# Twelve weight sets made by a fixed plan, and partial sums requested one job ahead, in a retention, GLU and expert kernel

## The chip, the cores and the metric

One core of one Trainium2 chip. The metric is the device time of one execution in microseconds (us). The kernel before has a median of 2044.2 us over three runs (2042.75 to 2045.66).

## The reference, cut to what matters

```
attn = (scale * q @ k.T * decay) @ v                    # 4 batches, 8 heads, 576 x 64
x = rmsnorm(attn rows) * rms_g                          # 2304 tokens x 512
x = (silu(x @ w_gate) * (x @ w_val)) @ w_out            # 512 -> 1536 -> 512
P = exp(x @ moe2_w_gate - max); 8 rounds of row and column scaling
out = sum over 8 experts e of P[:, e] * (relu(x @ w1[e]) @ w2[e])   # 512 -> 1024 -> 512
```

Everything is float32. A product of two float32 matrices is made of three TensorE products of fp32r halves: a value is split into `hi` (a cast on ScalarE) and `lo` (value minus `hi`, on VectorE or GpSimd), and hi x hi, hi x lo and lo x hi are summed in PSUM.

## The kernel before

There are three stages: retention (up to about 80 us), the gated layer (GLU) and the experts (from about 563 us to the end).

**GLU.** The 1536 hidden columns go in six sweeps (`s` = 0 to 5, lines 710 to 754), 256 columns each. A sweep runs over five blocks of tokens (`BLOCKS`: three of 512, two of 384), and a block is a generator of five steps `i` (`gated_block`, line 186): i = 0 gate of the first 128 columns and its silu (L203, ScalarE); i = 1 their val product, the multiply (L209, VectorE), the split of the result (`ghi` L210 on ScalarE, `glo` L211 on VectorE); i = 2 and i = 3 the same for the second 128 columns; i = 4 the output product (`x`), which TensorE does for the first 128 columns and then for the second, and its addition to `acc` (L232, VectorE). One step is twelve products in i = 0 to 3 and 24 in i = 4. After each step the loop lets other work put a piece into the queues: `step_weights` (the GLU's own weights) and `late_steps`.

**Late weight sets.** In the expert stage the weights are read from DRAM in a prepared form: seven 256-wide blocks (four of the matrix, sums and differences for a Strassen-like scheme of seven products), each as hi and lo. There are UJ = 32 such jobs per unit of tokens (8 experts x 4 pairs of column blocks), for w1 and for w2. Jobs 0 to 19 make theirs as they go. Those of jobs LATE = 20 to 31, twelve of them, are made during GLU sweeps by `late_weights` (line 666), which calls `prepared` (line 626), a generator of five steps: step 0 casts three raw blocks to hi in two staging buffers (`high`, L631, ScalarE); step 1 makes lo (L636, VectorE) and stores hi and lo to DRAM (L643, on SP's DMA queue); step 2 makes four sums and differences in place in the raw tile (L653, GpSimd); step 3 casts them into the same staging buffers; step 4 makes lo and stores (L640 or L643). After step 4 the raw tile is free, and the raw matrix of the next job is loaded into it (L668, SP's queue).

Call one turn of `late_steps` a place: 25 places in a sweep, five in a block. Before, the w1 generator (x) and the w2 generator (y) of a job take eight places: x at 0, 1, 2, 4, 5 and y at 2, 3, 4, 6, 7, and the next job starts eight places on. The loads lie at places 5 (x) and 7 (y), three places ahead of their use. While the plan starts a job in sweep 1, x and y share one pair of staging buffers; the second pair (`staging[2:4]`) belongs to GLU weights until that sweep is over. Twelve jobs end at place 95; `late_steps` is called in sweeps 1 to 4, 100 times.

**Experts.** Tokens go in three units of 768 (`u`), 32 jobs each (`n`). In unit 0 the first 20 jobs, which are five experts, work in another layout (token rows); their sums are stored in DRAM as six tiles `part_kept`. From job 20 on, jobs go through the loop at lines 162 onward of the last part (1162 to 1281), with an order written out by hand; results of the second layer are gathered transposed in `acc_d`. When a unit is over, `finish_unit` (line 1139) does one of its six 128-token tiles in each of the next six jobs (`next(finishing)`, line 1227): TensorE transposes four 128 x 128 blocks into the PSUM bank `qx` (L1144). For unit 0, SP requests the stored sum of that tile into `part`, a piece of the SBUF tile `o_second` (L1146), and VectorE adds it to the bank (L1152) into `st`; for unit 1 ScalarE copies the bank (L1156). SP stores `st` (L1157). A few products later in the same job, `first(m, 1)` (L1076) writes the bank `qx` again. VectorE, ScalarE, TensorE and SP each work in program order. On SP's queue a job has, in order, `load_w1(n + 1)` (line 1166), the pieces of `load_w2(n)` (L1056), the `part` load, the `st` store.

Of the kernel before, what the change touches and what calls it, by code (L numbers as in the profile page):

```python
# [43 lines left out]
NCH = UNIT // 128  # L44
NPAIR = FE // 256
UJ = E * NPAIR
ROUTED = NPAIR + 2
LATE = 20

@with_exitstack
def retention_glu_experts(ctx: ExitStack, tc: tile.TileContext, a, out):
# [6 lines left out]
    nc = tc.nc  # L60
# [24 lines left out]
    def f32(t):  # L85
        return t.bitcast(F32)


    sources, staging = [], []
# [160 lines left out]
    at, views = 0, []  # L250
# [190 lines left out]
    for pr in range(NP):  # L441
        for hh in (2 * pr, 2 * pr + 1):
            nc.gpsimd.tensor_mul(mask_rows[:, hh, :], causal, g_in[:, hh:hh + 1].to_broadcast([128, C]))
        step = steps[:, pr].rearrange("p (d c) -> p d c", c=NC)[:, :, 1:]
# [78 lines left out]
    jobs = [(u, e, g) for u in range(NU) for e in range(E) for g in range(NPAIR)]  # L523
    raw1, raw2 = {}, {}
    w1_kept = [kept.tile([128, 3584], F32, tag=f"w1_{n}", name=f"w1_kept{n}") for n in range(UJ)]
    w2_kept = [kept.tile([128, 3584], F32, tag=f"w2_{n}", name=f"w2_kept{n}") for n in range(UJ)]
    prob_kept = kept.tile([E, NT], F32, tag="prob_t", name="prob_kept")
    part_kept = [kept.tile([128, DM], F32, tag=f"part{t}", name=f"part_kept{t}") for t in range(NCH)]

    def load_job(n):  # L530
        if n < LATE:
            _, e, g = jobs[n]
# [90 lines left out]
            split(u, name, x, nc.gpsimd if name != "S2" else nc.vector)  # L623
            yield

    def prepared(n, a_n, dst, raw_tile, stages, order, places, signs):
        w = raw_tile.rearrange("p (b f) -> p b f", f=256)
        kept_n = dst.rearrange("p (s b f) -> p s b f", s=2, f=256)

        def high(i, blocks):  # L630
            nc.scalar.copy(stages[i][0][:, :blocks.shape[1] * 256].rearrange("p (b f) -> p b f", f=256), blocks)  # L631

        def low(i, blocks, at):
            size = blocks.shape[1] * 256
            hi, lo = (t[:, :size].rearrange("p (b f) -> p b f", f=256) for t in stages[i])
            nc.vector.tensor_sub(lo, blocks, f32(hi))  # L636
            for s, t in enumerate((hi, lo)):
                if at[-1] < at[0]:
                    for b, place in enumerate(at):
                        nc.sync.dma_start(kept_n[:, s, place, :], f32(t)[:, b, :])  # L640
                else:
                    step = at[-1] - at[0] or 1
                    nc.sync.dma_start(kept_n[:, s, at[0]:at[-1] + 1:step, :], f32(t))  # L643

        first, (pair_a, pair_b) = order
        high(0, w[:, 0:2, :])
        high(1, w[:, 2:3, :])
        yield
        low(0, w[:, 0:2, :], (first, first + 1))
        low(1, w[:, 2:3, :], (first + 2,))  # L650
        yield
        for o, x, y in signs:
            nc.gpsimd.tensor_sub(w[:, o, :], w[:, x, :], w[:, y, :])  # L653
        yield
        blocks = [w[:, p[0]:p[1] + 1:p[1] - p[0], :] for p in (pair_a, pair_b)]
        for i in range(2):
            high(i, blocks[i])
        yield
        for i in range(2):
            low(i, blocks[i], places[i])  # L660
        yield

    W1_SUMS = (0, ((0, 1), (2, 3))), ((3, 6), (4, 5)), ((0, 3, 0), (3, 2, 3), (2, 2, 0), (1, 1, 2))
    W2_SUMS = (4, ((0, 2), (1, 3))), ((3, 0), (1, 2)), ((2, 3, 2), (3, 1, 3), (1, 1, 2), (0, 0, 1))

    def late_weights():
        def load(t, src):
            nc.sync.dma_start(t, src)  # L668

        for n in range(LATE, UJ):  # L670
            _, e, g = jobs[n]
            if n == LATE:
                load(ahead_raw[0], a["w1"][e, g])
                load(ahead_raw[1], a["w2"][e, g])
                yield
            second_stage = staging[2:4] if now[0] > 1 else staging[:2]
            x = prepared(n, a["w1"], w1_kept[n], ahead_raw[0], staging[:2], *W1_SUMS)
            y = prepared(n, a["w2"], w2_kept[n], ahead_raw[1], second_stage, *W2_SUMS)
            more = n + 1 < UJ
            next(x)  # L680
            yield
            next(x)
            yield
            next(x)
            next(y)
            yield
            next(y)
            yield
            next(y)
            next(x)  # L690
            yield
            next(x)
            if more:
                load(ahead_raw[0], a["w1"][jobs[n + 1][1:]])
            yield
            next(y)
            yield
            next(y)
            if more:
                load(ahead_raw[1], a["w2"][jobs[n + 1][1:]])  # L700
            yield

    ahead_raw, now = [], [0]
    late_steps = late_weights()
    scored = logits()
    first_unit = first_operands(
# [2 lines left out]
    first_job = first_weights(0)  # L709
    for s in range(NSWEEP):  # L710
        last_sweep = s == NSWEEP - 1
        now[0] = s
        if s == 1:
            norm_pool.close()
            ahead = glu.enter_context(tc.tile_pool(name="ahead", bufs=1, side="right"))
            ahead_raw += [ahead.tile([128, 1024], F32, name="ahead_raw"), tp.tile([128, 1024], F32, tag="lg", name="ahead_raw_2", bufs=1)]
            staging += [(shared_tiles[0][:, 4096:], shared_tiles[1][:, 3072:]), (shared_tiles[1][:, 2048:2560], shared_tiles[1][:, 2560:3072]), *more_slots[:2]]
            next(late_steps)
        for j, (t0, n) in enumerate(BLOCKS):
            last = j == len(BLOCKS) - 1  # L720
            block = gated_block(s, t0, n, last, pmm, pac, hp, tp, 1 if last_sweep and last else KD, 512)
            first_norms = not s and j + 1 < B
            assert s or (t0 + n - 1) // S in normed
            for i in range(2 * SWEEP + 1):
                if last_sweep and last and i == 2 * SWEEP:
                    break
                if first_norms and j and not i:
                    next(norms[j + 1])
                if i == 2 * SWEEP:
                    step_weights()  # L730
                next(block)
                if first_norms:
                    for _ in range((1, 1, 1, 2, 0)[i]):
                        next(norms[j + 1], None)
                    if not j and i in (1, 2):
                        next(sums[B - 1], None)
                    if i == 2 * SWEEP - 1 and j + 2 < B:
                        next(norms[j + 2])
                if i == 2 * SWEEP or i < 2 and not first_norms or i == 2 and not s:
                    step_weights()  # L740
                if s and not last_sweep:
                    next(late_steps, None)
                if last_sweep and j and i % 2:
                    next(scored)
                if last_sweep and j == 1 and i == 2:
                    load_job(0)
                    load_job2(0)
                if last_sweep and j >= 3:
                    next(first_unit, None)
                    if j == 4:  # L750
                        next(first_job, None)
            else:
                for _ in block:
                    assert 0
# [381 lines left out]

    part = old[:, 3].rearrange("p h t -> p (h t)")[:, :DM]

    def finish_unit(u, banks, stages=None):
        for i, t in enumerate(reversed(range(NCH))):  # L1140
            ps = banks[i % len(banks)]
            at = u * UNIT + t * 128
            for k in range(KD):
                nc.tensor.transpose(ps[:, k * 128:(k + 1) * 128], acc_d[:, k, at:at + 128], ident)  # L1144
            if not u:
                nc.sync.dma_start(part, part_kept[t])  # L1146
            if stages:
                st = stages[i]
            else:
                st = ev.tile([128, 2, T], F32, tag="xs", name=f"st{u}_{t}").rearrange("p a b -> p (a b)")[:, :DM]  # L1150
            if not u:
                nc.vector.tensor_add(st, ps, part)  # L1152
            elif i % 2 and stages:
                nc.vector.tensor_copy(st, ps)
            else:
                nc.scalar.copy(st, ps)  # L1156
            nc.sync.dma_start(out[at:at + 128, :], st)  # L1157
            yield
# [3 lines left out]
    for n, (u, e, g) in list(enumerate(jobs))[LATE:]:  # L1162
# [6 lines left out]
        ahead = u + 1 < NU and (e, g) in ((E - 1, NPAIR - 3), (E - 1, NPAIR - 2))  # L1169
        turn = u + 1 < NU and (e, g) == (E - 1, NPAIR - 1)  # L1170
        begins = n % UJ == 0
        if g == NPAIR - 1:
            load_probs(n + 1)

# [108 lines left out]
    n, l = len(jobs) - 1, len(jobs) - 2  # L1283
# [24 lines left out]
    for j in (1, 0):  # L1308
        add_21(n, j)
    stages = [  # L1310
        ev.tile([128, 2, T], F32, tag="xs", name="st_xs").rearrange("p a b -> p (a b)"), old[:, 3].rearrange("p h t -> p (h t)"),
        prob_b[0], acc_d[:, 1, :UNIT], z.rearrange("p h t -> p (h t)"), prob_b[1],
    ]
# [78 lines left out]
```

## Time and profile before

| | us |
|---|---|
| median of three runs | 2044.2 |
| the profiled execution | 2043.37 |
| its span, first to last instruction | 2041.6 |
| TensorE busy in the span | 1988.1 |
| VectorE busy | 1497.0 |
| ScalarE busy | 917.3 |
| GpSimd busy | 816.7 |

How to read it: PE is TensorE's matmuls, PEld its weight loads, DVE VectorE, ACT ScalarE, POOL GpSimd, SP the engine that issues most DMAs. Times are us from the start of the span, `L1152` is line 1152. A row of waits reads: who waited, for whom, total us, times, longest. A row of a timeline reads: start, us, engine, line, operation, out<-in, count, and in brackets how long the engine was idle before and who ended that. A row of windows reads: stretch, its length, then busy us of PE, PEld, DVE, ACT and POOL (with counts), the granted TensorE clock (1.00 is 2.4 GHz, 0.50 is 1.2 GHz), the DMA engines' busy share, GB/s. A row of one line reads: count, duration in ns (min/median/max), first and last start. The sweeps are measured from the first multiply L209 of one to that of the next.

### The profile page before, as it was taken

To read this page: it belongs to the slowest core of one execution; us is meant where nothing else is said; L and a number is where in the kernel's file an instruction comes from. 1 tells how busy PE (TensorE), PEld (TensorE's weight loads), DVE (VectorE), ACT (ScalarE), POOL (GpSimd) and SP (SyncE) were. 2 spreads that over 40 slices of the span, in tenths; PEclk is the share of its full clock that TensorE was granted. 3 is DMA by queue.
4 is the path that set the end of the run, shared out by engine and by line. 5 is a ranking of instruction groups with operands and counts; after the bars stand their busy time and mean duration, and the time that the engine had idled before them with its cause. 6 is when DMAs were issued, how large, how long until landed. Compare 5 with 4: busy or idle time off the path is not lost.

```text
span 2041.6 us, 31093 instructions
## 1 busy us (share of the span) xinstructions
PE 1988.1 (97%) x11492; PEld 1870.2 (92%) x11492; DVE 1497.0 (73%) x2405; ACT 917.3 (45%) x1803; POOL 816.7 (40%) x770
## 2 busy tenths in 40 slices
PE   9999899999999999999998899999999999999998
PEld 7788778888889898989998899999999999999998
DVE  7856667775578777767785577777788777777777
ACT  4454334442355454444454344444455544444443
POOL 2301222221043445334564344545466545454543
PEclk9999899999999999999999899999999999999999
DMA  9414657662077888886766576767676776767673
GB/s 321 134 42 170 219 194 253 228 221 98 1 278 291 304 297 301 296 334 248 269 252 245 188 269 250 272 249 259 254 274 252 270 277 247 267 248 272 250 271 139
DMA packets 145511, 485.04 MB, mean 238 GB/s; under 512 B 15528, under 2 KB 54192, under 8 KB 128208
## 3 DMA queue, kind: packets, MB, share of 16 engines
q1 hardware_dynamic: 144064, 480.79, 64.9%
q8 instruction: 90, 1.47, 0.3%
q10 hardware_dynamic: 976, 1.23, 0.2%
q0 software_dynamic: 320, 1.05, 0.1%
q14 instruction: 61, 0.50, 0.1%
HBM read 359.20 MB, written 123.81 MB: 237 GB/s over the span
## 4 chain that ended last, share of the span: by engine, by line
PE 85%; DVE 6%; DMA 5%; ACT 1%; issue 1%; SPq 1%; POOL 0%; ACTq 0%; DVEq 0%
PE py L842 9%; PE pz L842 9%; PE px L842 9%; PE qz L1076 7%; PE qx L1076 7%; PE qy L1076 7%; PE gv L181 4%; PE gv L183 4%; PE gv L182 4%; PE qz L842 3%; PE y L183 3%; PE y L182 3%; PE y L181 3%; DMA o_second<-part_kept 2%; PE x L182 2%; PE e L1076 2%
## 5 line engine op out<-in xcount | busy, mean ns | idle before, releaser
L1258 POOL TENSOR_TENSOR o_second<-z,a_block 128x384 f32<-128x384 f32 x76 | 77.2, 1015 | 535.2 <-DVE z L1252 535.2
L842 PE MATMUL py<-sx,w1s 128*128 128x384 f32 x1152 | 234.7, 338 | 0.9 <-ACT py L1178 0.6
L1066 ACT CAST xhi<-o_second 128x384 fp32r<-128x384 f32 x380 | 187.6, 514 | 83.2 <-POOL o_second L1258 42.6
L1070 DVE TENSOR_TENSOR xlo<-o_second,xhi 128x384 fp32r<-128x384 f32 x230 | 217.1, 970 | 2.6 <-ACT xhi L1066 2.5
L842 PEld LDWEIGHTS py<-sx,w1s 128*128 128x128 f32 x1152 | 205.0, 190 | 4.5 <-ACT py L1178 2.5
L1070 POOL TENSOR_TENSOR xlo<-o_second,xhi 128x384 fp32r<-128x384 f32 x150 | 177.4, 1183 | 32.4 <-ACT xhi L1066 32.2
L842 PE MATMUL px<-xhi,w1s 128*128 128x384 f32 x640 | 189.1, 336 | 1.0 <-DVE t L209 1.0
L653 POOL TENSOR_TENSOR ahead_raw<-ahead_raw 128x256 f32<-128x256 f32 x96 | 78.1, 814 | 259.2 <-DVE w1s L636 191.1
L1087 DVE TENSOR_TENSOR acc<-acc,qz 128x384 f32<-128x384 f32 x290 | 158.7, 547 | 27.1 <-PE qz L1076 27.1
L1087 DVE TENSOR_TENSOR acc<-acc,qx 128x384 f32<-128x384 f32 x145 | 79.3, 547 | 85.1 <-PE qx L1076 85.1
L1097 ACT COPY qy<-qx 128x384 f32<-128x384 f32 x151 | 70.0, 464 | 131.2 <-PE qx L1076 93.9
L1105 ACT COPY qz<-qy 128x384 f32<-128x384 f32 x151 | 70.0, 463 | 129.6 <-PE qy L1076 123.1
L842 PEld LDWEIGHTS px<-xhi,w1s 128*128 128x128 f32 x640 | 117.9, 188 | 1.9 <-DVE t L209 1.3
L842 PE MATMUL pz<-sx,w1s 128*128 128x384 f32 x576 | 115.4, 334 | 0.0
L842 PE MATMUL pz<-xhi,w1s 128*128 128x384 f32 x384 | 113.7, 336 | 0.8 <-DVE z L1000 0.8
L842 PE MATMUL px<-xlo,w1s 128*128 128x384 f32 x320 | 107.0, 334 | 0.0
L842 PEld LDWEIGHTS pz<-sx,w1s 128*128 128x128 f32 x576 | 101.3, 188 | 0.7 <-issue 0.2
L1280 POOL TENSOR_TENSOR o_second<-o_second 128x384 f32<-128x384 f32 x76 | 101.3, 1332 | 0.0
L1279 POOL TENSOR_TENSOR o_second<-z 128x384 f32<-128x384 f32 x76 | 100.0, 1316 | 0.0
L181 PE MATMUL gv<-xhi,wslots 128*128 128x512 f32 (+1 forms) x260 | 96.4, 371 | 0.0
L183 PE MATMUL gv<-xhi,wslots 128*128 128x512 f32 (+1 forms) x260 | 95.6, 368 | 0.0
L182 PE MATMUL gv<-xlo,wslots 128*128 128x512 f32 (+1 forms) x260 | 95.6, 368 | 0.0
(381 smaller groups left out, 5868.5 us busy)
## 6 DMA issues: line engine op xcount, KB each, us to landing
w1s<-w_kept SPq DMA_DIRECT2D x76, 1792.0 KB, 7.3
w2s<-w_kept SPq DMA_DIRECT2D x38, 1024.0 KB, 7.0
w_kept<-w1s SPq DMA_DIRECT2D x20, 1792.0 KB, 6.6
w_extra<-w_kept SPq DMA_DIRECT2D x38, 768.0 KB, 7.6
rw<-in_w_dram SPq DMA_DIRECT2D x40, 512.0 KB, 5.5
w_kept<-xlo SPq DMA_DIRECT2D x40, 512.0 KB, 3.9
w2c<-w_kept SPq DMA_DIRECT2D x38, 512.0 KB, 8.0
w2c<-w_kept SPq DMA_DIRECT2D x76, 256.0 KB, 8.1
```

What stands on the lines that cost most here:

```text
L181: nc.tensor.matmul(ps, lhsT=lh, rhs=rh, start=start, stop=False)
L182: nc.tensor.matmul(ps, lhsT=lh, rhs=rl, start=False, stop=False)
L183: nc.tensor.matmul(ps, lhsT=ll, rhs=rh, start=False, stop=stop)
L653: nc.gpsimd.tensor_sub(w[:, o, :], w[:, x, :], w[:, y, :])
L842: nc.tensor.matmul(ps, lhsT=l, rhs=r[:, k, :], start=start and k == 0 and i == 0, stop=k == 1 and i == 2, skip_group_check=True,)
L1066: nc.scalar.copy(hi, x)
L1070: (engine or nc.vector).tensor_sub(lo, x, f32(hi))
L1076: nc.tensor.matmul(ps, lhsT=l, rhs=r, start=start and i == 0, stop=i == 2, skip_group_check=True)
L1087: nc.vector.tensor_add(dst, dst, ps)
L1258: nc.gpsimd.tensor_add(sums[0], z[:, 0, :], h_blocks[0])
L1279: nc.gpsimd.tensor_sub(sums[2], z[:, 1, :], z[:, 0, :])
L1280: nc.gpsimd.tensor_sub(sums[3], h_blocks[1], sums[1])
```

## The change

Two parts.

1. `late_weights` follows a table instead of an order of `yield`s. The first two jobs take x at places 0, 1, 2, 4, 5 and y at 7, 8, 9, 10, 11, with 13 places to the next job. The other ten take x at 0, 1, 2, 4, 5 and y at 5, 6, 7, 9, 10; three of them have 8 places to the next job, the rest 7. The first starts at place 2. Within a place the steps that free something come first (4, then 1, 3, 0, 2). Loads still follow step 4. From the third job on y uses the second pair of staging buffers. The last step is at place 104, and `late_steps` is also called in block 0 of the last sweep, 105 calls in all. Counted by sweep, the 120 steps lie 31, 31, 32, 26 and 0 in sweeps 1 to 5 before, and 18, 28, 34, 36 and 4 after. A load's lead over its use is 8 or 9 places for the second job, 8 (x) and 7 (y) for the third, 3 for the next three and 2 for the last six (before: 3 for all).
2. The first `part` load is issued at the head of job 32 instead of inside job 33, and each other one right after the addition that has read the buffer, a job ahead of its use.

```diff
+LATE_PLACES = (((0, 1, 2, 4, 5), (7, 8, 9, 10, 11)), ((0, 1, 2, 4, 5), (5, 6, 7, 9, 10)))
+LATE_CYCLES = (13, 13, 8, 8, 8, 7, 7, 7, 7, 7, 7, 7)
...
+    def late_plan():
+        plan, at = {}, 2
+
+        def put(place, rank, *what):
+            plan.setdefault(place, []).append((rank, *what))
+
+        for i, n in enumerate(range(LATE, UJ)):
+            for which, places in enumerate(LATE_PLACES[i >= 2]):
+                for step, place in enumerate(places):
+                    put(at + place, (3, 1, 4, 2, 0)[step], n, which, step)
+            at += LATE_CYCLES[i]
+        return plan, max(plan) + 1
+
     def late_weights():
...
+        plan, end = late_plan()
+        for place in range(end):
+            for _, n, which, step in sorted(plan.get(place, [])):
+                if not step:
+                    stages = staging[2:4] if which and n >= LATE + 2 else staging[:2]
+                    work[n, which] = prepared((w1_kept, w2_kept)[which][n], ahead_raw[which], stages, *(W1_SUMS, W2_SUMS)[which])
+                next(work[n, which])
+                if step == 4:
+                    load(which, n + 1)
             yield
...
-                if s and not last_sweep:
+                if s and not (last_sweep and j):
                     next(late_steps, None)
...
+    def load_part(t):
+        if t >= 0:
+            nc.sync.dma_start(part, part_kept[t])
+
     def finish_unit(u, banks, stages=None):
...
-            if not u:
-                nc.sync.dma_start(part, part_kept[t])
...
             if not u:
                 nc.vector.tensor_add(st, ps, part)
+                load_part(t - 1)
...
         begins = n % UJ == 0
+        if n == UJ:
+            load_part(NCH - 1)
```

## Rows read from the trace of the kernel before

**Rows 1.** The page: busy time by engine; granted clock in 40 slices.

```profile
PE 1988.1 (97%) x11492; PEld 1870.2 (92%) x11492; DVE 1497.0 (73%) x2405; ACT 917.3 (45%) x1803; POOL 816.7 (40%) x770
PEclk9999899999999999999999899999999999999999
```

**Rows 2.** The page: the chain that ended last, by line.

```profile
PE py L842 9%; PE pz L842 9%; PE px L842 9%; PE qz L1076 7%; PE qx L1076 7%; PE qy L1076 7%; PE gv L181 4%; PE gv L183 4%; PE gv L182 4%; PE qz L842 3%; PE y L183 3%; PE y L182 3%; PE y L181 3%; DMA o_second<-part_kept 2%; PE x L182 2%; PE e L1076 2%
```

**Rows 3.** Waits over the whole span: total us, times, longest.

```profile
DVE st L1152 <- DMA o_second<-part_kept: 25.1, 6, 5.3
...
PE qx L1076 <- DVE st L1152: 18.0, 6, 4.1
...
PE x L181 <- ACT ghi L210: 12.0, 5, 5.6
```

**Rows 4.** L1250, once a job: jobs 32-38, 64-70, and seven others.

```profile
L1250 DVE TENSOR_TENSOR z<-py,p x7: 556/556/558, 1070.2 to 1186.3; 128x384 f32<-128x384 f32 x7
...
L1250 DVE TENSOR_TENSOR z<-py,p x7: 556/558/558, 1565.6 to 1656.0; 128x384 f32<-128x384 f32 x7
...
L1250 DVE TENSOR_TENSOR z<-py,p x7: 556/558/558, 1200.9 to 1288.2; 128x384 f32<-128x384 f32 x7
```

**Rows 5.** Timeline in job 33, around the first addition of a stored sum.

```profile
1080.40 0.60 PE L1144 MATMUL qx<-ident,acc 128*128 128x128 f32 x4
1080.60 0.56 DVE L1221 SCALAR_TENSOR_TENSOR a_block<-px,prob_b 128x384 f32<-128x384 f32 x1 [1.30 <-PE px L842]
...
1085.23 0.69 DVE L1152 TENSOR_TENSOR st<-qx,o_second 128x512 f32<-128x512 f32 x1 [4.08 <-DMA o_second<-part_kept]
...
1085.98 0.45 PE L1076 MATMUL qx<-xhi,w2s 128*128 128x384 f32 x1 [2.89 <-DVE st L1152]
```

**Rows 6.** Line L1146, the six requests of stored sums.

```profile
L1146 SPq DMA_DIRECT2D o_second<-part_kept x6: 319/386/430, 1078.1 to 1175.2; - x6
...
DMA to landing us min/median/max: 7.0/7.7/8.8
```

**Rows 7.** Windows: sweeps 1 to 5 of the GLU, one row each.

```profile
169.40:257.00 87.60, 79.12 (x362) 67.89 (x361) 56.55 (x99) 34.68 (x64) 21.52 (x28) 0.94 0.63 206
257.00:337.40 80.40, 77.33 (x362) 66.47 (x361) 58.46 (x100) 34.65 (x66) 19.04 (x24) 0.98 0.66 217
337.40:416.70 79.30, 76.65 (x362) 66.97 (x361) 57.83 (x99) 33.58 (x64) 23.33 (x29) 0.98 0.73 239
416.70:490.70 74.00, 74.00 (x362) 65.54 (x361) 47.53 (x81) 27.22 (x51) 14.26 (x18) 1.00 0.57 188
490.70:564.00 73.30, 72.28 (x364) 59.12 (x363) 41.18 (x65) 26.64 (x45) 4.44 (x4) 1.00 0.03 11
```

**Rows 8.** Timelines of SP, ACT and PE, last block of sweep 1.

```profile
241.00 2.10 SPq L643 DMA_DIRECT2D w_kept<-w1s  x3
...
244.79 0.62 ACT L631 CAST sx<-ahead_raw 128x512 fp32r<-128x512 f32 x1 [3.71 <-DMA w_kept<-sx]
...
247.29 0.69 PE L181 MATMUL x<-ghi,wslots 128*128 128x384 f32 x1 [5.59 <-ACT ghi L210]
```

**Rows 9.** Timelines of SP, ACT and PE, last block of sweep 3.

```profile
398.83 0.40 SPq L668 DMA_DIRECT2D ahead_raw<-in_w_dram  x1
...
405.38 0.62 ACT L631 CAST sx<-ahead_raw 128x512 fp32r<-128x512 f32 x1 [3.20 <-issue]
...
406.77 0.44 PE L181 MATMUL x<-ghi,w_more 128*128 128x384 f32 x1 [1.79 <-ACT ghi L210]
```

**Rows 10.** Line L668, the 24 raw loads.

```profile
DMA to landing us min/median/max: 3.8/4.8/6.5
```

**Rows 11.** Windows at half clock: the first of seven stretches, and their sum.

```profile
213.30:216.70 3.40, 3.40 (x8) 2.65 (x9) 2.98 (x5) 0.00 (x0) 0.00 (x0) 0.51 0.60 211
...
sum 30.90, PE 26.95 PEld 25.03 DVE 19.79 ACT 5.61 POOL 6.09; mean PE 3.85 PEld 3.58 DVE 2.83 ACT 0.80 POOL 0.87
```

**Rows 12.** Costliest groups, 90 to 560 us: busy us, mean ns | idle before.

```profile
L636 DVE TENSOR_TENSOR w1s<-ahead_raw,sx 128x512 fp32r<-128x512 f32 x32 | 22.5, 702 | 2.4 <-ACT sx L631 2.4
```

More of the change, by code (lines that the diff above doesn't have):

```diff
@@ L624, in unit_operands, with prepared @@
             yield
-    def prepared(n, a_n, dst, raw_tile, stages, order, places, signs):
+    def prepared(dst, raw_tile, stages, order, places, signs):
         w = raw_tile.rearrange("p (b f) -> p b f", f=256)
@@ L664, in retention_glu_experts @@
     W2_SUMS = (4, ((0, 2), (1, 3))), ((3, 0), (1, 2)), ((2, 3, 2), (3, 1, 3), (1, 1, 2), (0, 0, 1))
-    def late_weights():
[L667 to L680, printed above, removed]
-            yield
[L682 to L701, printed above, removed]
@@ L703, in retention_glu_experts, with load @@
-    ahead_raw, now = [], [0]
+    def late_plan():
[8 more added lines that the diff above has]
+        return plan, max(plan) + 1
+    def late_weights():
+        def load(which, n):
+            if n < UJ:
+                nc.sync.dma_start(ahead_raw[which], a[("w1", "w2")[which]][jobs[n][1:]])
+        work = {}
+        for which in range(2):
+            load(which, LATE)
+        yield
+        plan, end = late_plan()
[7 more added lines that the diff above has]
+                    load(which, n + 1)
+            yield
@@ L704, in retention_glu_experts @@
+    ahead_raw = []
     late_steps = late_weights()
@@ L711, in retention_glu_experts @@
         last_sweep = s == NSWEEP - 1
-        now[0] = s
         if s == 1:
```

## The prediction

> **What bounds the kernel now.** I read the page first. TensorE is busy for 97% of the span, at a granted clock of full speed in nearly every slice [rows 1]: time can only be won where TensorE waits or runs at the lower clock. The chain that ended last [rows 2] is almost all products, but one DMA stands in it, the request of the stored sums, with 2% of the span. The waits [rows 3] give the causes: VectorE waits six times for those sums, 25.1 us in all, and TensorE six times for the addition behind them, 18.0 us. The other wait of TensorE of any size is for `ghi` in the GLU, 12.0 us in five waits. The change touches both places.
>
> Next I looked for stretches that do the same work without the wait. For the experts, one line that runs once a job is a ruler [rows 4]: from job 32 to job 38, which hold the six additions, six periods take 1186.3 - 1070.2 = 116.1 us. From job 64 to job 70, where unit 1 is finished in the same way, but with nothing to fetch, they take 1656.0 - 1565.6 = 90.4 us. Six plain periods take 87.3 us. For the GLU, the sweeps are five repetitions of the same products [rows 7]: 87.6, 80.4, 79.3, 74.0 and 73.3 us. In sweep 4 TensorE is busy for all 74.0 us at full clock, so 74.0 is the floor, and sweeps 1, 2 and 3 lose 13.6, 6.4 and 5.3 us, 25.3 us together.
>
> The clock is part of these losses. There are seven stretches at half speed (1.2 instead of 2.4 GHz), of 30.9 us together [rows 11]; four lie in the GLU and three among the stored sums, each during a wait of TensorE of 1.8 us or more or right after it, and three of the six waits for stored sums are followed by none. A stretch of 3.4 us at half speed loses 1.7 us of products. The two rulers include this, so I work with them and don't add clock and waits.
>
> **The stored sums (part 2 of the change).** In job 33 the request goes out at 1078.1 us and lands 7.0 us later (median of the six 7.7 [rows 6]), since SP issues it inside the job, behind the pieces of the w2 load. Meanwhile the transposes were over at 1081.0 and VectorE's last work before the addition at 1080.60 + 0.56 = 1081.2; the addition starts at 1085.2 and TensorE, which wants the bank back, stands still for 2.89 us until 1086.0 [rows 5]. After the change the buffer has been filled a job earlier, 14.6 us ahead (87.3 / 6), about twice the 7.7 us that a request needs. The addition can then run from 1081.2 to 1081.9 (0.69 us), and TensorE asks for the bank at 1086.0 - 2.89 = 1083.1: 1.2 us to spare. So the wait should go altogether, and what is late next is nothing in this job.
>
> Size: 116.1 - 90.4 = 25.7 us. From below 18.0 us, the bare waits, if the clock came back at no gain; from above 116.1 - 87.3 = 28.8 us, which would make six jobs with 24 transposes as short as plain ones. I take **25.7**, since jobs 65 to 70 do the same transposes and differ only in the engine that empties the bank.
>
> Costs of this part. The requests are as many as before, six. The first is now issued at the head of job 32, behind `load_w1(33)` and ahead of the w2 pieces, which start one issue (0.39 us [rows 6]) later; those feed products of the next job, over 10 us on, so nothing pays. The others wait on SP for the addition; behind them is the `st` store, which waited for the same addition before, and then the next job's loads, in the same place as before. The store goes out 0.39 us later, and its tile is written again only a job later. I cost all this at nothing; if the cover were gone it would be 0.4 us a job, 2.4 us.
>
> **The plan for the weight sets (part 1).** What it removes is seen in sweep 1 [rows 8]: x and y of a job share staging buffers there, and each store is followed one place later by a cast into the buffer that it reads. At 241.0 SP issues three stores, the cast must wait 3.71 us for one of this step's, it holds up the `ghi` behind it in ScalarE's queue, and TensorE stands still for 5.59 us. ScalarE's order makes step i = 2 the sensitive one: behind it comes `ghi` of the second half, which the output product needs one product set later; a cast that is late in i = 3 or i = 4 has the whole output product to hide in.
>
> - Sweep 1 goes from 31 steps of late work to 18, and no buffer is used again earlier than two places after its store. A place is some 2.7 us in a block of 512 (74.0 us over 27 units, an output product being two, shorter blocks three quarters) and two are more than the 3.8 us from that store at 241.0 to the cast at 244.8. I take 74.5: a gain of **13**.
> - Sweep 2 goes from 31 to 28 steps, with w1 and w2 of the fourth job apart, which before were not. A wait of a cast at i = 2 caused most of the loss there. I take 75.4: a gain of **5**.
> - Sweep 3 goes from 32 to 34 steps. Its loss came from a load, not a store [rows 9]: issued at 398.8, it landed with the cast at 405.38, 6.5 us later, three places after, in a block of 384, and TensorE waited 1.79 us. That cast falls on another step now, but the last six jobs have only two places of lead, and loads take 3.8 to 6.5 us [rows 10]. Two places are about 4.1 us in a block of 384 and 5.4 in one of 512. So ScalarE will wait for raw data about every second time. Most of these casts fall on i = 3, 4, 0 (by the plan, ten of the twelve with two places' lead are at i = 1, 3, 4 or 0), where a wait of 2 us is hidden; the two at i = 2 are both in sweep 4. I take no change: **0**.
> - Sweep 4 goes from 26 to 36 steps and has nothing to lose before. Two sensitive casts of about 1 us of wait for TensorE: I take a loss of **2**.
> - Sweep 5 gets four steps in its first block. Two of them are VectorE's, two operations of at most 0.70 us each [rows 12], 2.8 us. VectorE is busy for only 41.2 of 73.3 us there [rows 7]: nothing; 2.8 us if that cover were gone.
>
> Part 1 is 13 + 5 + 0 - 2 = **16 us**. Its bounds: at best all 25.3 us; at worst sweeps 3 and 4 each lose 5.6 us more than I say, as much as the longest wait there is, so 5.
>
> **Sum.** 25.7 + 16 = 41.7 us. The profiled execution took 2043.4 (span 2041.6), 0.8 under the median of 2044.2. 2043.4 - 41.7 = 2001.7 against its own time, and **2002.5** against the median.
>
> **The rivals.**
> A. *The short leads bite.* In sweeps 3 and 4 a load has two places instead of three, and these sweeps carry more stores (DMA engines are busy for 0.73 and 0.57 of them now [rows 7]; with 34 and 36 steps for 32 and 26 both come to about 0.78). For it: the load of [rows 9], for which even three places were too few. Against it: the casts with short leads are nearly all at steps that hide a wait. If six of the twelve cost TensorE 1.8 us and half of them a stretch at half speed (1.7), that is 6 x 1.8 + 3 x 1.7 = 16 us: part 1 comes to about 18 - 16 = 2 us, the time to 2044.2 - 25.7 - 2 = 2016. The Trainium skill speaks for this rival: its page "DMA: Bandwidth & Descriptors", section "Latency and other measured facts", gives HBM's latency as 0.2 us on average and 2 us at high load. By it each of the twelve loads could be up to 1.8 us later, an estimate of at most 21.6 us, and the time at most 2024. The loads of the trace, from 3.8 to 6.5 us, do spread by more than that already.
> B. *Part 1 gains everything*: sweeps 3 and 4 also run at the floor, 25.3 us. 2044.2 - 25.7 - 25.3 = 1993. For it: sweep 4 does so now with 26 steps. Against it: it is to have 36.
> C. *The addition stays late*: only the bare waits go, or part of them, since VectorE's queue or the transposes come last in its place. 2044.2 - 18 - 16 = 2010. The 1.2 us to spare speak against it, and so do jobs 65 to 70.
> D. *Slower.* The mechanism of A at its worst, at the raw loads of the last six jobs: each of the twelve as dear as the worst wait of the GLU, 5.59 us and 1.7 us of lost clock, 7.3 x 12 = 88 us, against 18 + 25.7 won: 2044.2 + 44 = 2088. It decides from 43.7 / 12 = 3.6 us a load; the one such wait seen cost 1.79 and a stretch at half clock, and i = 2 has two of them.
> E. *The change does not do what it says*: steps left over at the end, or a first request held on SP. The plan ends at place 104 and there are 105 calls; nothing ahead of the request in SP's queue is late. Part 1 alone would be 2028.
>
> **How the numbers follow.** Forecast 0.74, A 0.12, B 0.05, C 0.06, D 0.01, E 0.02. Part 1 between 5 and 25 and part 2 between 22 and 27 us give 1993 to 2017 at the far ends; I give **1994 to 2014**, which leaves out most of A, D, E and a little of B. This kernel's measurement can tell about 0.2%, 4.1 us, from no change; all cases but D lie below 2040: faster 0.97, same 0.02, slower 0.01.
>
> **What would show it.** Right: no wait of VectorE for the stored sums, the ruler of jobs 32 to 38 at about 90.4 us, sweep 1 under 76 us with no wait for stores, sweep 2 about 75, fewer stretches at half speed. Wrong: casts waiting for raw loads and TensorE behind `ghi` in sweeps 3 and 4 (A, D), which would stand there over 80 us; a wait of TensorE for L1152 that stays (C); late work after block 0 of the last sweep (E).

## The result, and the profile after

The changed kernel takes **2009.47 us** (median of four runs, 2006.1 to 2012.98) against 2043.59 for the kernel before (four runs, 2042.75 to 2045.66): a ratio of 0.9832, 95% interval 0.9813 to 0.985, 34.1 us faster. The forecast was 2002.5, its range 1994 to 2014. So the direction and the range were right, and the time is 7.0 us above the forecast.

The profiled execution of after took 2009.68 us, its span is 2007.9, 33.7 less than before's. The first look is at the page: TensorE's busy time and the chain by line, the rows that answer to [rows 1, 2].

```profile
PE 1977.3 (98%) x11492; PEld 1864.5 (93%) x11492; DVE 1504.2 (75%) x2405; ACT 918.0 (46%) x1803; POOL 817.2 (41%) x770
...
PE py L839 10%; PE pz L839 10%; PE px L839 10%; PE qx L1073 8%; PE qz L1073 8%; PE qy L1073 8%; PE gv L183 4%; PE gv L185 4%; PE gv L184 4%; PE qz L839 4%; PE y L185 3%; PE y L184 3%; PE y L183 3%; PE x L184 2%; PE x L185 2%; PE x L183 2%
```

The DMA of the stored sums is gone from the chain's lines. The waits of after, to be held against [rows 3]:

```profile
ACT w_more L633 <- DMA ahead_raw<-in_w_dram: 7.7, 3, 4.0
...
PE x L183 <- ACT ghi L212: 7.7, 4, 3.5
...
ACT sx L633 <- DMA ahead_raw<-in_w_dram: 6.8, 3, 4.6
```

No row of VectorE waiting for the stored sums is left, and none of TensorE waiting for that addition. The wait of TensorE for `ghi` is smaller (7.7 for 12.0 us) but still there, four times. And ScalarE's casts (L633, before L631) now wait for raw loads of the weight sets; in before the profile names no such wait, though the cast of [rows 9] stood 3.20 us until its load had landed.

The ruler of [rows 4] in after, jobs 32 to 38 (the first seven starts of that line in the stretch):

```profile
L1252 DVE TENSOR_TENSOR z<-py,p x7: 557/558/558, 1062.2 to 1152.7; 128x384 f32<-128x384 f32 x7
```

1152.7 - 1062.2 = 90.5 us for six periods, against 116.1 before: part 2 brought 25.6 us, what it was said to bring. The rest is in the sweeps. Windows of sweeps 1 to 5 of after, in the columns of [rows 7]:

```profile
171.20:245.20 74.00, 74.00 (x362) 65.54 (x361) 49.72 (x88) 29.83 (x56) 12.17 (x16) 1.00 0.45 150
245.20:322.50 77.30, 75.09 (x362) 65.39 (x361) 59.06 (x100) 32.72 (x62) 16.96 (x21) 1.00 0.63 207
322.50:405.40 82.90, 77.95 (x362) 68.19 (x361) 59.73 (x99) 34.87 (x67) 24.97 (x30) 0.96 0.71 235
405.40:482.50 77.10, 74.86 (x362) 65.31 (x361) 55.45 (x91) 31.61 (x61) 24.62 (x31) 1.00 0.77 254
482.50:556.00 73.50, 72.44 (x365) 59.28 (x364) 42.56 (x67) 27.76 (x47) 4.86 (x5) 1.00 0.12 43
```

| sweep | before [rows 7] | forecast | after | change |
|---|---|---|---|---|
| 1 | 87.6 | 74.5 | 74.0 | -13.6 |
| 2 | 80.4 | 75.4 | 77.3 | -3.1 |
| 3 | 79.3 | 79.3 | 82.9 | +3.6 |
| 4 | 74.0 | 76.0 | 77.1 | +3.1 |
| 5 | 73.3 | 73.3 | 73.5 | +0.2 |

Part 1 is worth 13.6 + 3.1 - 3.6 - 3.1 = 10.0 us, not 16. With 25.6 that makes 35.6; the spans differ by 33.7, since in these two executions the first GLU multiply starts at 92.0 us in after and at 90.2 before. The stage ahead of it is not touched by the change, and that start lies anywhere from 89.7 to 94.3 us in the runs below, so these 1.8 us are not counted as the change's. The moved steps of the last sweep cost nothing: from the start of sweep 5 to job 20 it is 401.2 us before and 401.3 after.

**Where TensorE still stops.** TensorE stops in four places of sweeps 2 to 4. The timeline of after around the longest stop, in sweep 3 (rows of SP, VectorE, ScalarE and TensorE, in order of time):

```profile
370.71 0.64 SPq L684 DMA_DIRECT2D ahead_raw<-in_w_dram  x1
...
377.08 0.62 ACT L633 CAST sx<-ahead_raw 128x512 fp32r<-128x512 f32 x1 [1.86 <-DMA ahead_raw<-in_w_dram]
...
377.91 0.48 ACT L205 ACTIVATE t<-gv 128x384 f32<-128x384 f32 x1
...
378.68 0.55 DVE L211 TENSOR_TENSOR t<-t,gv 128x384 f32<-128x384 f32 x1
...
379.26 0.51 ACT L212 CAST ghi<-t 128x384 fp32r<-128x384 f32 x1 [0.86 <-DVE t L211]
...
379.82 0.69 PE L183 MATMUL x<-ghi,w_more 128*128 128x384 f32 x1 [3.50 <-ACT ghi L212]
```

Read it backwards: TensorE waits 3.50 us for `ghi`, `ghi` for VectorE's multiply, the multiply for the silu (L205; the lows of the same set, which stand ahead of it on VectorE, end 0.4 us later), and the silu stands in ScalarE's queue behind the cast, which waits 1.86 us for a load issued 6.4 us earlier (377.08 - 370.71). This is job 27's w1 at place 66: i = 1 of a block of 384, two places of lead. A stretch at half speed follows (1.2 GHz: granted clock 0.50; windows of after):

```profile
379.50:386.30 6.80, 6.37 (x19) 5.97 (x20) 5.25 (x9) 1.90 (x4) 2.64 (x3) 0.50 0.33 116
```

The stop in sweep 4 (job 30's w2, place 92, i = 2, again in a block of 384), timeline of after:

```profile
455.93 0.40 SPq L684 DMA_DIRECT2D ahead_raw<-in_w_dram  x1
...
460.26 0.93 ACT L633 CAST w_more<-ahead_raw 128x512 fp32r<-128x512 f32 x2 [3.36 <-DMA ahead_raw<-in_w_dram]
...
461.66 0.44 PE L183 MATMUL x<-ghi,w1s 128*128 128x384 f32 x1 [2.09 <-ACT ghi L212]
```

The stop in sweep 2 has no transfer in it. VectorE's timeline, and TensorE's row behind it:

```profile
295.06 0.68 DVE L137 SCALAR_TENSOR_TENSOR cv<-raw,cv 128x512 int32<-128x512 int32 x1
...
297.06 0.69 DVE L638 TENSOR_TENSOR w1s<-ahead_raw,sx 128x512 fp32r<-128x512 f32 x1
297.66 0.68 DVE L638 TENSOR_TENSOR w1s<-ahead_raw,w1s 128x512 fp32r<-128x512 f32 x1
298.26 1.02 DVE L638 TENSOR_TENSOR w_more<-ahead_raw,w_more 128x512 fp32r<-128x512 f32 x2
299.20 0.55 DVE L211 TENSOR_TENSOR t<-t,gv 128x384 f32<-128x384 f32 x1
...
300.35 0.44 PE L183 MATMUL x<-ghi,w1s 128*128 128x384 f32 x1 [1.34 <-ACT ghi L212]
```

VectorE is never idle here: the GLU's own weight chain (L137) and the lows of two weight sets stand ahead of the multiply, in a block of 384 where the products last three quarters as long. The fourth stop has the same shape: in the last block of sweep 3, again of 384, the lows of two sets (job 27's w1 and w2) stand right ahead of the multiply. Timelines of after, VectorE and TensorE:

```profile
394.50 1.02 DVE L638 TENSOR_TENSOR w_more<-ahead_raw,w_more 128x512 fp32r<-128x512 f32 x2
395.44 0.55 DVE L211 TENSOR_TENSOR t<-t,gv 128x384 f32<-128x384 f32 x1
...
396.59 0.45 PE L183 MATMUL x<-ghi,w_more 128*128 128x384 f32 x1 [0.77 <-ACT ghi L212]
...
397.60 0.44 PE L184 MATMUL x<-glo,w_more 128*128 128x384 f32 x1 [0.57 <-DVE glo L213]
```

Sweep 3 lies 8.9 us above the floor of 74.0. Its stops (3.50, 0.77 and 0.57) and the half of 6.8 us that the lower clock costs make 8.2 of them.

In contrast, the longest wait of a cast hurts nobody (timeline of after, i = 3 of the last block of sweep 3; TensorE has no stop beside it):

```profile
401.18 0.62 ACT L633 CAST sx<-ahead_raw 128x512 fp32r<-128x512 f32 x1 [4.64 <-DMA ahead_raw<-in_w_dram]
```

### The profile page after: what moved, and what is told of

It reads as the page before. It is cut to its first block, busy times and chain, and to the rows that moved or that the text cites. A ratio compares the mean times of both kernels' runs of the same rounds, so it can differ in the third digit from the quotient of the medians.

```text
span 2007.9 us, 31095 instructions
## 1 busy us (share of the span) xinstructions
PE 1977.3 (98%) x11492; PEld 1864.5 (93%) x11492; DVE 1504.2 (75%) x2405; ACT 918.0 (46%) x1803; POOL 817.2 (41%) x770
## 3 DMA queue, kind: packets, MB, share of 16 engines
q10 hardware_dynamic: 976, 1.23, 0.2%
## 4 chain that ended last, share of the span: by engine, by line
PE 89%; DVE 5%; DMA 3%; ACT 1%; issue 1%; POOL 0%; SPq 0%; ACTq 0%; DVEq 0%; POOLq 0%
PE py L839 10%; PE pz L839 10%; PE px L839 10%; PE qx L1073 8%; PE qz L1073 8%; PE qy L1073 8%; PE gv L183 4%; PE gv L185 4%; PE gv L184 4%; PE qz L839 4%; PE y L185 3%; PE y L184 3%; PE y L183 3%; PE x L184 2%; PE x L185 2%; PE x L183 2%
## 5 line engine op out<-in xcount | busy, mean ns | idle before, releaser
L1260 POOL TENSOR_TENSOR o_second<-z,a_block 128x384 f32<-128x384 f32 x76 | 77.2, 1016 | 510.7 <-DVE z L1254 510.7
L1063 ACT CAST xhi<-o_second 128x384 fp32r<-128x384 f32 x380 | 188.2, 516 | 83.6 <-POOL o_second L1260 42.4
L655 POOL TENSOR_TENSOR ahead_raw<-ahead_raw 128x256 f32<-128x256 f32 x96 | 79.2, 825 | 268.6 <-DVE w_more L638 100.2
L1084 DVE TENSOR_TENSOR acc<-acc,qx 128x384 f32<-128x384 f32 x145 | 79.5, 548 | 82.6 <-PE qx L1073 82.6
```

The lines of the kernel that those rows point to most:

```text
L1063: nc.scalar.copy(hi, x)
L1084: nc.vector.tensor_add(dst, dst, ps)
L1260: nc.gpsimd.tensor_add(sums[0], z[:, 0, :], h_blocks[0])
```

## The experiments

Each was compared with the kernel before on the same chip; "after" in a diff is the changed kernel. Four runs each, medians.

**1. The two parts apart.** Part 1 alone, from after:

```diff
+            if not u:
+                load_part(t)
...
                 nc.vector.tensor_add(st, ps, part)
-                load_part(t - 1)
...
-        if n == UJ:
-            load_part(NCH - 1)
```

> The plan for the weight sets alone; the stored sums requested inside the job as before. If the two parts are independent, the time is the changed kernel's 2009.5 plus the 25.7 us of the six additions, 2035, and the ruler of jobs 32 to 38 is back at 116 us. If part 1 were worth the 16 us of the prediction it would be 2043.6 - 16 = 2027.6.

2035.7 us (2032.6 to 2040.69), ratio 0.9953 (0.9937 to 0.9969). Part 2 alone is before with `load_part` and its two calls, as in the change:

```diff
-                nc.sync.dma_start(part, part_kept[t])
...
                 nc.vector.tensor_add(st, ps, part)
+                load_part(t - 1)
...
+        if n == UJ:
+            load_part(NCH - 1)
```

> The early requests alone, with the weight sets made as before. Independent parts: 2043.6 - 25.7 = 2018, with the sweeps at 87.6, 80.4, 79.3 and 74.0 us as before and the ruler of jobs 32 to 38 at 90.4 us. If the requests' gain were only the bare waits: 2043.6 - 18 = 2025.6.

2017.01 us (2016.28 to 2020.85), ratio 0.9863 (0.9848 to 0.9877). The rulers of the two:

```profile
L1251 DVE TENSOR_TENSOR z<-py,p x7: 558/558/559, 1064.9 to 1183.6; 128x384 f32<-128x384 f32 x7
```

```profile
L1255 DVE TENSOR_TENSOR z<-py,p x7: 557/558/559, 1068.7 to 1159.2; 128x384 f32<-128x384 f32 x7
```

118.7 us with the late requests, 90.5 with the early ones. By the ratios, against 2044.2, part 1 is worth 9.6 us (6.3 to 12.9) and part 2 28.0 (25.1 to 31.1); the sum, 37.6, agrees with the 34.1 of both within those intervals. The shortfall of the forecast lies in part 1 alone.

**2. Are the late loads the loss?** From after, the loads of the last six jobs are left out:

```diff
         def load(which, n):
-            if n < UJ:
+            if n < LATE + 6:
```

> The changed kernel without the raw loads of the last six of the twelve jobs (w1 and w2 of jobs 26 to 31 are then made from what lies in the raw tiles), so that no cast waits for a load with a lead of two places; all other steps and stores stay. Theory short lead: the waits of TensorE of 3.5 us at 376 us and of 2.1 us at 460 us go with their stretch at half clock; sweep 3 falls from 82.9 to about 76 us, sweep 4 from 77.2 to about 74.5, together 9 us: 2000. Theory density (VectorE's and ScalarE's queues are too full in sweeps 3 and 4, and stores come back late): sweeps 3 and 4 stay within 2 us of what they are, 2008 or more.

2000.41 us (2000.11 to 2007.14), ratio 0.9786 (0.9769 to 0.9802): about 9 us under after. The profiled execution is the longest of the four (2007.14), so only its sweeps are read. Sweeps 3 and 4 of it, by windows, and the row that answers to after's stop of 3.50:

```profile
325.80:405.70 79.90, 76.68 (x362) 67.09 (x361) 59.63 (x99) 35.37 (x68) 26.98 (x32) 0.98 0.64 220
405.70:480.10 74.40, 74.40 (x362) 65.44 (x361) 53.88 (x91) 30.52 (x59) 21.92 (x29) 1.00 0.59 204
...
381.14 0.45 PE L183 MATMUL x<-ghi,w_more 128*128 128x384 f32 x1 [1.53 <-ACT ghi L212]
```

Sweep 4 is within 0.4 us of the floor, as the theory of the short lead said. Sweep 3 is 3.0 us shorter, but at 79.9 and not at 76: of the stop of 3.50 us 1.53 stay with no load in it, and the fourth stop stays whole (0.77 and 0.57 us, at 396.87 and 397.89). So of the 12.0 us by which these two sweeps of after lie above the floor, 5.7 go with the loads in this profile (2.7 of 3.1 in sweep 4, 3.0 of 8.9 in sweep 3); by the medians 9 us go. The loads (the transfers, and the casts that wait for them) are nearly all of the loss of sweep 4, and a third of that of sweep 3.

**3. Eight places a job, so three places of lead.** From after; the plan gets longer by five places, so the last sweep takes late steps in three blocks instead of one, and the first two score tiles move to another buffer:

```diff
-LATE_CYCLES = (13, 13, 8, 8, 8, 7, 7, 7, 7, 7, 7, 7)
+LATE_CYCLES = (13, 13, 8, 8, 8, 8, 8, 8, 8, 8, 8, 8)
...
-                if s and not (last_sweep and j):
+                if s and not (last_sweep and j > 2):
```

> The changed kernel with eight places to the next job for all of the last ten, so that every load has three places of lead and sweeps 3 and 4 have 31 steps each; the plan then ends at place 110, in block 2 of the last sweep, and the logits of the first two blocks use another buffer. Theory short lead: sweep 4 near 74.5, sweep 3 below 79 us, together 5 to 8 us less, about 2003. Theory density: less as well, by the ratio of steps (34 to 31, 36 to 31), about half of the 12 us lost there: 2004, but the waits that go are VectorE's and ScalarE's own, not those for loads. If neither: the steps now fall on other places with as many bad ones, 2009.

**1999.17 us** (1998.15 to 2000.2), ratio 0.9772 (0.9756 to 0.9789): the fastest version here (version 3 from here on), about 10 us under after. Sweeps 2 to 4 by windows, and its longest wait for a load, on ScalarE's timeline:

```profile
242.80:321.30 78.50, 76.48 (x362) 66.99 (x361) 58.98 (x99) 32.64 (x62) 16.91 (x21) 0.98 0.62 203
321.30:397.60 76.30, 75.65 (x362) 65.36 (x361) 58.26 (x96) 33.72 (x64) 23.02 (x27) 1.00 0.74 246
397.60:471.70 74.10, 74.10 (x362) 65.47 (x361) 49.88 (x84) 29.43 (x57) 19.79 (x26) 1.00 0.67 225
...
425.93 0.62 ACT L635 CAST sx<-ahead_raw 128x512 fp32r<-128x512 f32 x1 [4.58 <-DMA ahead_raw<-in_w_dram]
```

Sweeps 3 and 4 lose the 9.6 us that after has more (82.9 + 77.1 - 76.3 - 74.1). Five of the casts of the last twelve sets still wait for their load, 10.5 us in all (after: eight, 20.0), and the longest is about as long as any in after; none of them stops TensorE. The fourth stop of after is gone too, though it had no load in it. This run changes three things at once: the lead, the step on which each piece falls, and the number of steps in sweeps 3 and 4 (31 and 31 in place of 34 and 36).

> The eight-place plan unaltered, as the reference on this chip: ratio 0.977 to 0.979.

2000.44 us (1998.89 to 2003.09), ratio 0.9772 (0.9748 to 0.9795), in another set of runs; sweeps 2 to 4 are 78.2, 75.7 and 74.6.

**4. After itself once more**, beside the runs that follow:

> The changed kernel unaltered, on the chip of the runs beside it, as their reference: ratio 0.983 to the kernel before as measured, whatever the theory. If the parts overlap (each alone gains less or more than in company), its time should differ from before minus the two parts' own gains, 10.1 and 28.8 us, by over 3 us.

2010.15 us (2009.25 to 2013.96), ratio 0.9835 (0.9817 to 0.9853). Sweeps 1 to 4 are 74.0, 77.3, 83.6 and 77.1, and TensorE stops in the same four places. Only their sizes differ: the stop of 3.50 is 2.98 here, and the fourth is 1.91 instead of 0.77, since the cast of job 27's w2 ahead of it (place 71, i = 1) waits 2.35 us for its load, in after 0.33.

**5. Is it the lead?** Version 3 with each load issued one place later, so two places of lead and the casts on the same steps:

```diff
+        due = []
         for place in range(end):
+            for which, n in due:
+                load(which, n)
+            due = []
...
-                    load(which, n + 1)
+                    due.append((which, n + 1))
```

> The eight-place plan of the run before, with each raw load issued one place later, so that the lead is two places and the number of steps in a sweep stays. Theory short lead: casts at i = 2 in blocks of 384 (places 92 and 97, in sweep 4) and at i = 1 (places 41, 76, 81) wait for raw data and TensorE stops some 2 us at two to four of them: 4 to 8 us above the eight-place plan, sweep 4 at 77 or more. Theory density: the lead is not what matters, within 2 us of the eight-place plan.

1999.79 us (1998.4 to 2002.38), ratio 0.9783 (0.9768 to 0.9797): no loss, where 4 to 8 us were expected. It is a weaker test than it was meant to be: measured from the start of sweep 3, nine of the twelve loads of the last six jobs went out within 0.8 us of where they did in version 3, and three 1.2, 2.5 and 3.7 us later. Still six casts waited 15.2 us for their loads, three quarters of the 20.0 in after (one of them 1.77 us at i = 1, but of a block of 512), and TensorE stopped for 0.68 us at most in sweeps 3 and 4. Sweep 3 is 76.5 us, and sweep 4 stayed at the floor:

```profile
400.50:474.50 74.00, 74.00 (x362) 65.42 (x361) 50.58 (x84) 29.43 (x57) 21.05 (x27) 1.00 0.69 230
```

**6. Is it the step?** After, with job 30's w2 one place later in its first three steps (cast, lows, sums): its cast moves from i = 2 to i = 3. Its load is issued where it was, so the lead of this load grows from two places to three at the same time.

```diff
+                if (n, which) == (30, 1):
+                    places = (6, 7, 8, 9, 10)
```

> The changed kernel with the first three w2 steps of job 30 one place later: its cast leaves i = 2 of a block of 384 (place 92) for i = 3 (place 93). Everything else, the leads of the other loads and the steps per sweep too, stays. Theory step: what costs is not that ScalarE waits for a load but at which step; the stop of 2.1 us at 460 goes, sweep 4 falls from 77.2 to about 74.5, 2.5 us less than the changed kernel. Theory lead or density: the stop only moves, sweep 4 stays within 1 us of 77.

2008.7 us (2007.81 to 2009.43), ratio 0.9809 (0.9783 to 0.9836). Sweep 4 by windows and the cast on ScalarE's timeline:

```profile
407.50:482.20 74.70, 74.37 (x361) 65.14 (x360) 56.82 (x91) 31.84 (x61) 25.72 (x31) 1.00 0.79 259
...
462.32 0.93 ACT L633 CAST w_more<-ahead_raw 128x512 fp32r<-128x512 f32 x2 [2.01 <-DMA ahead_raw<-in_w_dram]
```

TensorE has no stop there any more, and sweep 4 falls from 77.1 to 74.7. That is what the step theory expected, but the wait is shorter too, 2.01 us in place of 3.36, and a wait of 2 us is free at i = 2 as well: in the repeat of version 3 the cast of job 30's w1 falls on the same place 92, waits 1.96 us, and TensorE idles 0.15. ScalarE's and TensorE's timelines of that run:

```profile
452.09 0.62 ACT L635 CAST sx<-ahead_raw 128x512 fp32r<-128x512 f32 x1 [1.96 <-DMA ahead_raw<-in_w_dram]
...
454.08 0.44 PE L184 MATMUL x<-glo,w1s 128*128 128x384 f32 x1 [0.15 <-DVE glo L213]
```

So this run doesn't tell the step from the shorter wait. That the step counts is seen in after itself: 3.36 us at i = 2 cost 2.09, and 4.64 us at i = 3, in a block of 384 as well, cost nothing. In the medians 2.4 us are too few to stand out of after's own spread (6.9 us).

**7. VectorE's queue as the cause in sweep 3.** After, with the first lows of job 27's w1 moved from i = 2 to i = 3:

```diff
+                if (n, which) == (27, 0):
+                    places = (0, 2, 2, 4, 5)
```

> The changed kernel with one step moved by one place: the first w1 lows of job 27 go from i = 2 (place 67) to i = 3 (place 68), behind the multiply in VectorE's queue. Its load, its cast at i = 1 and that cast's wait for the load stay. Theory VectorE's queue: the late load reaches TensorE at 376 us not through ScalarE but because the lows, which need the cast, stand ahead of the multiply; the stop of 3.5 us falls to under 1 us, the stretch of 6.8 us at half clock with it, sweep 3 from 82.9 to about 77: 2004. Theory lead (ScalarE's queue, which holds the silu behind the cast): the stop stays at 2 us or more and sweep 3 above 80.

2009.39 us (2007.8 to 2011.33), ratio 0.9832 (0.9816 to 0.9848), no gain; sweep 3 is 82.6 us. The timeline of it at that place:

```profile
376.86 0.62 ACT L633 CAST sx<-ahead_raw 128x512 fp32r<-128x512 f32 x1 [1.76 <-DMA ahead_raw<-in_w_dram]
377.69 0.48 ACT L205 ACTIVATE t<-gv 128x384 f32<-128x384 f32 x1
...
378.21 0.55 DVE L211 TENSOR_TENSOR t<-t,gv 128x384 f32<-128x384 f32 x1 [3.76 <-ACT t L205]
...
379.36 0.69 PE L183 MATMUL x<-ghi,w_more 128*128 128x384 f32 x1 [3.16 <-ACT ghi L212]
```

VectorE now idles 3.76 us until the silu, and TensorE stops nearly as before (3.16 us): the wait goes through ScalarE. That VectorE's queue was at fault in this stop is a theory of mine that fell.

**8. The stop that is left in version 3** (sweep 2, VectorE's queue) was taken on in two ways: job 23 shifted by one place, and job 23's w2 begun in the same place with its other early steps one place later.

```diff
-LATE_CYCLES = (13, 13, 8, 8, 8, 8, 8, 8, 8, 8, 8, 8)
+LATE_CYCLES = (13, 13, 9, 7, 8, 8, 8, 8, 8, 8, 8, 8)
```

> The eight-place plan with one job one place later (cycles 9 and 7 in place of two of 8), so that the w1 lows and the w2 lows of that job no longer stand at i = 1 and i = 2 of one block of 384 ahead of the multiply in VectorE's queue. Theory VectorE's queue: the stops of 1.3 and 0.6 us in sweep 2, seen in every kernel with the new plan, go, and with them a stretch at half clock where it follows: sweep 2 from 78.5 to about 75.5 us, 2 to 3.5 us less in all. Rival, that stop comes from a cast waiting or from the load: it stays or moves, 0 to 1 us.

```diff
+                if (n, which) == (23, 1):
+                    places = (5, 7, 8, 9, 10)
```

> The eight-place plan with the w2 steps 1 to 3 of job 23 one place later, so that the w2 lows stand at i = 3, behind the multiply, and only the w1 lows ahead of it. Theory VectorE's queue: the stops of 1.3 and 0.6 us in sweep 2 go, none takes their place, sweep 2 falls to about 75 us: 1997 for a kernel before of 2044. Rival: the stop is due to the weights' own steps on VectorE and half of it stays, 1998 to 1999.

2000.28 us (1999.39 to 2001.16) and 2001.44 (1998.01 to 2001.8), ratios 0.9784 (0.9769 to 0.9798) and 0.9771 (0.9748 to 0.9795): no gain over version 3. Each removes or shrinks the stop near 297 and gets another at 311 to 313, of 1.21 and 1.44 us; sweep 2 is 76.5 and 77.2 us. Timeline of the first of them at the new stop:

```profile
306.30 3.56 POOL L657 TENSOR_TENSOR ahead_raw<-ahead_raw 128x256 f32<-128x256 f32 x4 [2.08 <-DVE w1s L640]
...
308.31 0.96 DVE L131 TENSOR_SCALAR cv<-cv 128x512 f32<-128x512 f32 x1
...
313.14 0.44 PE L183 MATMUL x<-ghi,w1s 128*128 128x384 f32 x1 [1.21 <-ACT ghi L212]
```

The stop has only moved along VectorE's queue, to a multiply of the next block of 384.

## Why the prediction was right, and where it was off

- **Stored sums, 25.7 us: right**, by the step given. The ruler reads 90.5 us where 90.4 was said, the two waits are gone, and nothing else became late in these jobs, so C (2010, the addition late for another cause) is out although its time is near the measured one. The cost of nothing for the moved requests held too.
- **Sweep 1, 13 us: right** (13.6), with the floor of 74.0 reached and TensorE never stopped in it; so was nothing for the last sweep.
- **Sweep 3, taken as 0: the step that failed.** It measured 3.6 us of loss. The lead was read correctly (casts wait for loads about every second time; eight of twelve did, two of them for 0.33 us only), but the step went on: "at i = 1, 3, 4 or 0), where a wait of 2 us is hidden". At i = 1 of a block of 384 it wasn't. Behind that cast in ScalarE's queue stands the silu of the second half, whose multiply and `ghi` come two steps later. The cast's wait of 1.86 us is part of a stop of 3.50, with a stretch at half clock behind it; without the load 1.53 stay, so the load costs about 2.0 of it. I had looked only at the `ghi` behind i = 2. The 1.53 us, and the fourth stop with its lows of two sets on VectorE, have no load in them, and I didn't price them either. Before's own sweep 3 is no fixed mark: it was 76.8 us in the run with part 2 alone, which leaves the sweeps as they were.
- **Sweep 2, 5 us: mis-sized**, 3.1. The stores' waits went as said; what was left out altogether is VectorE's queue: two sets' lows ahead of the multiply in a block of 384. The stop has the VectorE rows of L638 directly in front of L211. Experiment 8 bears this out: where these lows are moved, the stop near 297 goes or shrinks and another comes.
- **Sweep 4, a loss of 2: about right** (3.1), in part by luck. Two casts at i = 2 were to cost about 1 us each. The one in a block of 512 waited 0.33 us and cost nothing; the one in a block of 384 waited 3.36 and stopped TensorE by 2.09. The other 1.0 us of the 3.1 shows in no stop of over 0.5 us.
- **Sum.** 13.6 + 3.1 - 3.6 - 3.1 = 10.0 for part 1 in place of 16: six of the seven microseconds missed. The last is within what one execution differs from another. (The range's far end should read 1992 and not 1993 by its own bounds, 25 and 27; nothing hangs on it.)
- **The rivals.** B (1993) needed sweeps 3 and 4 at the floor; they lie 12.0 us above it. D and E did not come. A (short leads bite, 2016) had the right mechanism and too large a size: two of twelve casts reached TensorE, in the repeat of after three, not six. The HBM latency that the prediction cited from the Trainium skill, page "DMA: Bandwidth & Descriptors", section "Latency and other measured facts", did not show as later loads: after's raw loads, on the row of line L684, land in

```profile
DMA to landing us min/median/max: 3.7/4.4/6.4
```

against 3.8, 4.8 and 6.5 before [rows 10], at a DMA share of 0.71 and 0.77 in sweeps 3 and 4. It was the lead that shrank, not the transfer that grew.

**Left open.** What gives version 3 its 10 us: the longer lead, the other steps or the smaller number of steps in sweeps 3 and 4. Without the transfers the time falls as far (experiment 2). But the fourth stop, which has no load in it, stays there and is gone in version 3, so the lead is not all of it. Experiment 5 didn't separate lead and step, because nine of twelve issue times barely moved, nor did experiment 6, which changed both; no run changed the number of steps alone. And what keeps 1.53 us of the stop in sweep 3 when there is no load: VectorE's operations there run slowly beside GpSimd's sums (see the last section), but no run took those sums away.

## What to carry to other kernels

When background work is spread over the steps of a pipelined loop, check what stands behind each piece in its engine's queue, up to the next product that waits. In blocks of the same length, a wait of 4.6 us for a transfer cost nothing at one step; at the step before it 3.4 us cost 2.1 and 2.0 us nothing; and 1.9 us cost about 2.0 at a third, where the queues were late already. Price each step by the shortest block in which it falls, and for every engine that the piece uses, not only for the one that waited in the old profile. The densest plan was not the best one here: one more place a job, with the last steps moved into a later sweep, was worth 10 us, though it is not shown by which of its effects. And a transfer that a later addition needs is best requested as soon as its buffer is read, which was worth 25.6.

## What the runs showed of the hardware that was not expected

- **VectorE next to GpSimd.** In after, the L131 on VectorE takes 0.41 to 0.43 us in the 31 cases in which GpSimd does nothing beside it, and 0.76, 0.96 and 0.97 in the three that meet GpSimd's sums (L655). The L137 takes 0.68 to 0.69 in 27 cases alone; of the five that meet the sums four take 1.22 or 1.23, and one 0.70. The L131 of experiment 8, shown above beside GpSimd's four sums, takes 0.96. Examples from VectorE's and GpSimd's rows of after (the sums last from 371.44 to 375.16):

```profile
295.66 0.42 DVE L131 TENSOR_SCALAR cv<-cv 128x512 f32<-128x512 f32 x1
...
373.34 1.23 DVE L137 SCALAR_TENSOR_TENSOR cv<-raw,cv 128x512 int32<-128x512 int32 x1
...
371.44 3.72 POOL L655 TENSOR_TENSOR ahead_raw<-ahead_raw 128x256 f32<-128x256 f32 x4 [14.63 <-DVE w_more L638]
```

  The L137 of the example and the L131 of experiment 8 each lose some 0.54 us. The Trainium skill, page "SBUF — State Buffer", section "SBUF: two separate sides", names a port pair that these two engines share; that VectorE is slower beside GpSimd agrees. That this port is the cause is not shown by any run.
- **The lower clock follows a short stop in some executions and not in others.** Before, the stretches at half speed lay at waits of 1.8 us or more. Here the same stop of about 1.3 us near 297 to 301 is followed by 3.4 us at half speed (granted clock 0.51) in the profiles of experiments 2, 3 (both times), 5 and 6, and by none in those of after, its repeat, part 1 alone and experiment 7. Windows of version 3:

```profile
299.30:302.70 3.40, 3.40 (x12) 3.40 (x11) 2.42 (x5) 0.00 (x0) 1.29 (x2) 0.51 0.94 334
```

  That is 1.7 us of products, and it makes sweep 2 of version 3 78.5 us where after has 77.3, with the same work in it. What decides it stays open.
- **One kernel's runs spread by several us.** After's four runs lie 6.9 us apart and those of its repeat 4.7; before's four lie 2.9 apart, but in the sets of seven beside the experiments 2.7 to 9.1. The gain of one small edit is better read from its sweep in the trace than from the median.
